# A planned delta-net and FFN kernel: the same steps in another order

## The chip, the cores and the metric

The kernel runs on one core of one Trainium2 chip. The core has five engines, each with its own instruction queue: TensorE (PE in the profile; its weight loads are PEld), VectorE (DVE), ScalarE (ACT), GpSimd (POOL) and SyncE (SP, which issues most of the DMA transfers). The engines run at their own pace [...]. The metric is the device time of one execution in microseconds, from the first instruction to the last.

## What is computed

Two blocks follow each other. The first is a delta-rule attention over q, k, v (batch 4, 8 heads, 768 tokens, 48 features):

```
k_n = k / (norm(k) + 1e-6)
for t in range(768):
    y[t]  = q[t] @ state
    state = state + beta[t] * outer(k_n[t], v[t] - k_n[t] @ state)
```

Its output, as 3072 tokens of 384 features, goes through a multiplicative feed-forward block:

```
a = x @ w1;  b = x @ w2          # 384 -> 1024
h = (a * b) @ w3                 # 1024 -> 1024
out = h @ w_out                  # 1024 -> 384
```

The weights arrive as 64-bit floats, so each has to be turned into a 32-bit one on the chip.

## The kernel before

**Attention.** The 768 steps are cut into 12 chunks of 64 tokens. Within a chunk the recurrence is solved at once through the inverse of a triangular 64x64 matrix for each of the 32 batch-heads. The work of a chunk m is cut into parts, each named by a letter and the number: `k`, `q`, `v`, `p` load (`p` loads k and q in blocks of 32 tokens, 16 DMAs in two steps); `K`, `Q` (chunks 0 and 1, on TensorE) and `d` (later ones, on VectorE) transpose; `g`, `N` compute norms and weights for a pair of chunks; `s` computes scores (L360, L366), U and the masked PT; `u` sends U to DRAM in blocks; `V` (for a pair of chunks) fetches the blocks and inverts all 32x32 ones by 31 steps on VectorE (L434, L439), then stores them; `e` fetches them back and fills the corner of the 64x64 inverse (L473 and L487 on TensorE, each followed by a copy on ScalarE); `n` scales v on GpSimd; `c` is the chain from one chunk's state to the next, three products in L517 (CH1, CH2, CH3) whose results VectorE turns into R, X and the new state S; `y` computes the outputs (L618), which ScalarE copies to xT, and for odd chunks six small DMAs (L650, "xTfix") move the last head pair in xT.

**Weights.** `P0` to `P7` are pieces of w_out, `P8` to `P23` of w3, `P24` to `P29` of w1, `P30` to `P35` of w2. Each piece is loaded by SP into one of five buffers, then handled by three ScalarE instructions (L671 to L673), one of VectorE (L675, the "shift") and two of GpSimd (L677, L678). Since (a * b) @ w3 @ w_out is linear in a * b, the kernel multiplies w3 and w_out once: `t` transposes a piece of w3 (L713), `f` folds eight of them with w_out into one block of w34 (L722, two halves). w_out lies in the memory that w2 fills later, so w2's pieces wait for the folds.

**Feed-forward.** For each pair of chunks (u = 0 to 5), `a<u><j>` computes block j of a and of b (L742, three matmuls each of 128x512), copies a on ScalarE, multiplies on VectorE (L756) into one of ten slabs; `o<u><b>` sums eight blocks with w34 into 128 output rows (L762), copies them (L768) and stores them (L771).

**Order.** Nothing is scheduled by the compiler. A list of names, `ORDER` (L37), is walked from left to right: each name advances its part by one step, and a step issues the instructions of one engine. `in_text_order` (L155) then chains the instructions of each engine, so that every queue runs strictly in the order of the list. The buffers are also handed out in list order: `two_banks` (L142) gives the two double banks of PSUM to scores, chain and outputs in turn, `bank` (L145) three banks to transposes, folds, `a` and `o`. While `V0` and `V1` run, one of the double banks is held for them.

Large TensorE phases are those with 128x128 weights (L713, L722, L742, L762); small ones address the array in tiles (64x48, 48x64, 32x32: L360, L366, L473, L487, L517, L618).

```
    for name in ORDER.split():
        step(name)
    in_text_order()
```

## Time and profile before

611.39 us is the median of three runs (611.04 to 615.68). The profiled execution spans 610.1 us.

| | us |
|---|---|
| TensorE busy | 567.9 (93%) |
| VectorE busy | 322.0 (53%) |
| ScalarE busy | 183.2 (30%) |
| GpSimd busy | 145.3 (24%) |
| L742 (a and b), both weights, x576 | 262.6 |
| L762 (outputs), x384 | 127.1 |
| L722 (folds), x128 | 46.8 |
| DMA traffic | 55.67 MB, 91 GB/s in the mean |

The chain that ended last is 83% TensorE, 5% SP issuing, 4% DMA. In the rows of forty digits each digit is the busy share of 15.25 us in tenths. The idle time of an engine that is not on the chain costs nothing by itself.

The order of time is: the first loads and transposes (to about 25 us), the first weights and block inverse (to 53), the folds with the chain of chunks 0 and 1 between them (53 to 131), then `a` and `o` with the attention of later chunks in between, and from 538 us feed-forward alone.

### The profile page before, as it was taken

Reading aid. Unit: us, or ns where it says so; the run is one execution under the profiler, and the core shown is the slowest. Engines: PE = TensorE matmul, PEld = TensorE weight load, DVE = VectorE, ACT = ScalarE, POOL = GpSimd, SP = SyncE. Lnnn points to the kernel's source line nnn. Section 1 sums busy time; section 2 is a strip of 40 time slices with the busy share of each in tenths; the row PEclk is TensorE's granted clock in tenths of the full one; section 3 lists DMA queues with packets and bytes.
Section 4 is the critical chain, followed back from the end, with each engine's and each line's share of the span. In section 5 each row is a group of like instructions: output and inputs, shape, how many; then the busy total and the mean of one; then the engine's idle time right before and its main releaser. Section 6 shows DMA issues by size and latency. Waiting matters only on the chain.

```text
span 610.1 us, 17982 instructions
## 1 busy us (share of the span) xinstructions
PE 567.9 (93%) x7804; PEld 333.7 (55%) x7804; DVE 322.0 (53%) x752; ACT 183.2 (30%) x373; POOL 145.3 (24%) x150
## 2 busy tenths in 40 slices
PE   3736988999899999999999999999999999999997
PEld 2724667644565655655466655465564655644454
DVE  1569875697665955557946449556386123100110
ACT  2776667654530212402111302122121212211100
POOL 6489866575242101100130000112001000000000
PEclk9999997899999999999999999999999999999999
DMA  9668887867755255253356324551321300000001
GB/s 216 163 207 195 195 176 168 193 118 155 158 77 105 67 116 85 30 94 72 62 119 87 55 55 96 101 74 23 57 81 26 97 2 2 24 30 13 1 13 39
DMA packets 202223, 55.67 MB, mean 91 GB/s; under 512 B 192352, under 2 KB 195424, under 8 KB 202144
## 3 DMA queue, kind: packets, MB, share of 16 engines
q1 hardware_dynamic: 197952, 53.74, 42.0%
q10 hardware_dynamic: 4192, 0.79, 0.9%
q8 instruction: 61, 1.00, 0.7%
q14 instruction: 18, 0.15, 0.1%
HBM read 42.30 MB, written 11.01 MB: 87 GB/s over the span
## 4 chain that ended last, share of the span: by engine, by line
PE 83%; SPq 5%; DMA 4%; ACT 3%; DVE 2%; issue 1%; POOL 1%; ACTq 0%; POOLq 0%; DVEq 0%
PE ps_f L742 38%; PE ps_f L762 20%; PE ps_f L722 5%; PE ps_w L517 5%; PE ps_w L618 4%; PE ps_t L473 2%; PE ps_w L366 2%; PE ps_t L487 2%; PE ps_w L360 2%; SPq L226 2%; PE ps_f L713 1%; SPq L663 1%; DMA X<-in_q_dram 1%; DMA raw<-in_moe_w_out_dram 1%; DMA ktok<-in_k_dram 1%
## 5 line engine op out<-in xcount | busy, mean ns | idle before, releaser
L742 PE MATMUL ps_f<-xT,w1s 128*128 128x512 f32 x288 | 131.1, 600 | 1.5 <-DMA xT<-xT 1.5
L742 PE MATMUL ps_f<-xT,w2s 128*128 128x512 f32 x288 | 131.5, 600 | 0.5 <-DVE ab L756 0.5
L762 PE MATMUL ps_f<-w,ab 128*128 128x384 f32 x384 | 127.1, 488 | 0.1
L756 DVE TENSOR_TENSOR ab<-a,ps_f 128x512 f32<-128x512 f32 x48 | 32.6, 683 | 136.5 <-PE ps_f L742 135.6
L762 PEld LDWEIGHTS ps_f<-w,ab 128*128 128x128 f32 x384 | 72.3, 190 | 51.5 <-issue 3.3
L742 PEld LDWEIGHTS ps_f<-xT,w2s 128*128 128x128 f32 x288 | 53.0, 190 | 61.2 <-issue 57.6
L742 PEld LDWEIGHTS ps_f<-xT,w1s 128*128 128x128 f32 x288 | 53.0, 190 | 60.4 <-issue 55.0
L751 ACT COPY a<-ps_f 128x512 f32<-128x512 f32 x48 | 27.7, 585 | 148.3 <-PE ps_f L742 116.5
L266 POOL TENSOR_TENSOR sq<-ktok 128x384 f32<-128x384 f32 x24 | 20.2, 844 | 147.7 <-DVE ss L268 82.1
L768 ACT COPY osb<-ps_f 128x384 f32<-128x384 f32 x24 | 11.5, 479 | 126.0 <-PE ps_f L762 97.0
L503 POOL TENSOR_TENSOR vtok<-vtok,n 128x384 f32<-128x384 f32 x24 | 20.2, 858 | 117.0 <-DMA vtok<-in_v_dram 103.9
L439 DVE TENSOR_TENSOR Vb<-Vb,tb 128x31 f32<-128x31 f32 (+15 forms) x124 | 45.2, 364 | 4.3
L722 PE MATMUL ps_f<-w2s,w3T 128*128 128x384 f32 x128 | 46.8, 518 | 0.1
L434 DVE TENSOR_TENSOR tb<-Vb,Ub 128x31 f32<-128x31 f32 (+15 forms) x124 | 43.9, 354 | 4.6 <-DMA Ub<-Ud 0.7
L639 ACT COPY xT<-ps_w 48x256 f32<-48x256 f32 x96 | 30.5, 366 | 48.4 <-PE ps_w L618 31.9
L722 PEld LDWEIGHTS ps_f<-w2s,w3T 128*128 128x128 f32 x128 | 24.9, 202 | 16.3 <-issue 2.7
L366 PE MATMUL ps_w<-KQ 48*64 48x64 f32 x768 | 31.3, 241 | 0.0
L360 PE MATMUL ps_w<-KQ 48*64 48x128 f32 x384 | 30.6, 307 | 0.7 <-ACT PT L386 0.7
L360 PEld LDWEIGHTS ps_w<-KQ 48*64 48x64 f32 x384 | 25.3, 154 | 8.6 <-issue 6.6
L713 PE MATMUL ps_f<-ident,w 128*128 128x128 f32 x64 | 12.6, 335 | 17.9 <-POOL w L678 17.9
L366 PEld LDWEIGHTS ps_w<-KQ 48*64 48x64 f32 x768 | 28.7, 154 | 0.3 <-issue 0.2
L581 DVE TENSOR_TENSOR S<-S,ps_w 48x768 f32<-48x768 f32 x20 | 19.0, 950 | 9.7 <-PE ps_w L517 9.5
(94 smaller groups left out, 642.4 us busy)
## 6 DMA issues: line engine op xcount, KB each, us to landing
raw<-in_moe_w_dram SPq DMA_DIRECT2D x16, 512.0 KB, 5.5
vtok<-in_v_dram SPq DMA_DIRECT2D x24, 192.0 KB, 4.0
raw<-in_moe_w_dram SPq DMA_DIRECT2D x24, 192.0 KB, 4.2
out_dram<-osb SPq DMA_DIRECT2D x24, 192.0 KB, 2.0
ktok<-in_k_dram SPq DMA_DIRECT2D x44, 96.0 KB, 3.4
raw<-in_moe_w_out_dram SPq DMA_DIRECT2D x8, 384.0 KB, 4.8
Ud<-U SPq DMA_DIRECT2D x48, 64.0 KB, 2.0
Ub<-Ud SPq DMA_DIRECT2D x6, 512.0 KB, 3.4
```

The lines of the kernel that those rows point to most:

```text
L360: pe.matmul(ps[half(z), 0, n : n + 128], lhsT=x[:, 0, :], rhs=x.rearrange("p j t -> p (j t)"), start=True, stop=True,)
L366: pe.matmul(ps[half(z ^ j), 1, n + C * j : n + C * j + C], lhsT=x[:, 0, :], rhs=x[:, j, :], start=True, stop=True,)
L434: dve.tensor_tensor(out=tv, in0=V[:, 0 : s + 1, s : s + 1].to_broadcast([P, s + 1, n]), in1=U[:, s, s + 1 : BS].unsqueeze(1).to_broadcast( ...
L439: dve.tensor_tensor(out=o, in0=o, in1=tv, op=ALU.subtract)
L517: pe.matmul(out(ps, r, h, z), lhsT=lhs(r, h, z), rhs=rhs(r, h, z), start=True, stop=True,)
L618: i = pe.matmul(region(h, z, r), lhsT=lhs, rhs=rhs, start=part[n] not in part[:n], stop=part[n] not in part[n + 1 :],)
L639: act.copy(out=xT[f, p:NP:2, b : b + NR, cc, :].rearrange("p a r t -> p r a t"), in_=pyv[f, z, b : b + NR],)
L722: pe.matmul(ps[:, 0:DM], lhsT=w3Ts[jc, kc // 4][:, kc % 4 * P : kc % 4 * P + P], rhs=wo[:, kc], start=(kc == 0), stop=(kc == KF - 1),)
L742: pe.matmul(ps[:], lhsT=w[:, m, js], rhs=x[:, m].rearrange("p b c t -> p (b c t)"), start=(m == 0), stop=(m == KM - 1),)
L751: act.copy(out=a[:], in_=ps[:])
L756: dve.tensor_tensor(out=t[:], in0=a[:], in1=ps[:], op=ALU.mult)
L762: pe.matmul(ps[:, 0:DM], lhsT=abs_[u, jc][:, b * P : (b + 1) * P], rhs=w34[:, jc, :], start=(jc == 0), stop=(jc == KF - 1),)
```

## The change

Only `ORDER` is replaced. The new list holds the same names the same number of times, so no instruction is added, removed or altered; each engine's queue, and with it the turn of every buffer, comes in another order. It is meant to put small TensorE phases more often beside each other, so that the array changes between large and small matmuls less often, and to bring weight pieces and loads in an order that suits the opening better. P1, P0 and P6 are now loaded before `k1` (before: P7 alone), and eleven pieces before the blocks of chunk 0 (`u0`), where there were eight.

The lists up to the first step of `c1` before and a similar stretch after, and their ends:

```diff
-P7 k0 g0 q0 V0 K0 g0 g0 k1 K0 K0 P7 P7 P7 K0 K0 Q0 Q0 Q0 Q0 Q0 g0 g0 g0 g0 K1 P0 P0 P0 P0 g0
-P3 K1 K1 K1 P3 P3 s0 g0 beta beta g0 P1 P1 q1 P1 beta N0 s0 K1 Q1 Q1 Q1 P10 P3 s0 s0 Q1 Q1
-P1 p2 s0 s0 s0 P10 P10 P10 P6 P6 s1 s1 s1 P11 s1 s1 s1 P6 P6 P13 N0 u0 u1 P11 P11 P12 P2 s1
-d2 d2 t2 t2 P13 P13 N0 P11 P13 V0 V0 P2 P2 P23 V0 P12 P12 t5 P12 P2 P22 P23 P4 V0 P22 V0 V0
-V0 V0 V0 P22 V0 V0 V0 t5 V0 P23 P4 P4 t3 t3 k3 t4 P22 t4 t14 t14 f2 P23 f1 P4 V0 V0 V0 V0 P5
-P5 P5 v0 P20 P20 V0 V0 V0 V0 V0 t15 P5 f2 V0 V0 P21 P21 f1 f2 P20 n0 n0 f7 V0 V0 V0 V0 P21
-V0 V0 V0 P15 P15 P15 V0 f1 V0 V0 t15 p3 P14 P14 s0 P20 k2 t12 f7 P17 t12 P14 f7 P21 t13 g1
-g1 P15 f6 p2 d2 d2 g1 V0 V0 V0 t7 t13 d3 t7 P17 f6 f6 P14 g1 g1 g1 P18 t6 t6 P18 s2 e0 P17
-g1 g1 f3 e0 g1 g1 N1 e0 P16 e0 P18 P16 s2 s2 s2 e1 e1 s2 s2 e0 f3 P16 e0 c0 c0 P9 P19 P19
-P19 f3 P9 P9 P17 t9 t9 p3 P18 t10 t10 v1 y0 y0 e1 e1 P16 t8 t8 d3 d3 P8 d3 s3 s3 s3 P9 P8
-P26 P26 s3 s3 s3 u2 P24 t1 t1 u3 c0 c0 P19 t11 P8 n1 n1 N1 N1 P24 e1 P25 V1 P26 P26 c1 f5
+k0 K0 g0 K0 P1 P0 g0 g0 q0 P6 k1 P1 K0 P0 Q0 K0 g0 P3 beta P6 K0 P1 V0 Q0 P0 Q0 K1 P1 g0 Q0 P6
+Q0 q1 P3 P7 g0 P10 P3 g0 K1 beta K1 K1 P7 g0 P6 K1 beta g0 P10 p2 Q1 g0 P3 P7 s0 P10 Q1 N0 P0
+s0 P2 Q1 Q1 Q1 P23 P7 s0 P2 P10 P12 s1 P13 s1 s0 s1 s0 s0 P2 P11 s1 P2 P12 s1 N0 u0 d2 s1 P13
+P12 u1 P23 s0 v0 P23 P11 t2 V0 d2 P12 P23 P22 P13 P13 V0 N0 P11 P4 k2 t2 t5 t4 P11 V0 V0 V0 V0
+P5 t3 V0 P22 V0 t5 V0 V0 P22 t4 V0 V0 P4 P20 t15 V0 P21 n0 f2 P4 V0 P5 P5 t3 P22 k3 t14 t15 V0
+P4 P20 V0 f1 P14 V0 P21 P20 V0 P15 P5 P21 V0 g1 f2 P14 V0 t14 f2 V0 V0 f1 P20 P18 V0 P15 p3 P14
+V0 t12 P19 P15 P21 V0 f1 V0 V0 f7 P14 P9 t6 P15 t12 n0 f7 P18 t13 V0 V0 t6 V0 V0 P8 V0 f7 V0 V0
+t7 g1 p2 t13 t7 V0 V0 P18 P8 g1 V0 g1 f3 d3 g1 s1 P17 g1 e0 P8 d2 f6 g1 P9 e1 f3 g1 P9 d2 d3 g1
+P18 s2 e0 g1 P19 N1 e0 s2 P16 e1 P8 f6 P9 P17 s2 P19 e0 e0 p3 f6 s2 f3 e0 s2 t10 s0 s2 c0 d3
+P19 s1 e1 v1 t10 d3 t1 P16 t1 s3 c0 n1 n1 s3 P16 y0 s3 t11 e1 y0 e1 s3 P25 P25 s3 t0 P24 P17 c0
+f5 V1 s3 u2 t11 u3 c0 P26 P17 P25 c1 V1 t0 P24 P16 P25 P24 V1 t9 e1 c1 f5 V1 V1 c1 k4 f5 c1 V1
...
-y11 o42 o42 o42 o43 o43 o43 a57 a57 a57 a57 a56 a56 a52 a52 a53 a53 a50 a50 o41 a50 a52 a52
-o41 o41 a50 a56 a56 a51 a51 a55 a53 a55 a53 a54 a54 a54 a54 a55 a55 a51 a51 o53 o53 o53 o51
-o51 o51 o52 o52 o50 o50 o50 o52
+c11 a45 a45 a42 a46 a45 a44 a45 a46 a44 c11 c11 o40 y11 o42 o40 o43 o32 y11 o43 y11 a53 o40 o43
+o42 a53 a54 o41 a54 a53 a53 a51 o41 o42 a51 a57 a57 a51 a51 a50 a54 a50 a57 a54 a55 a52 a57 a56
+a55 a56 a50 o41 a52 a56 a50 a55 a55 a56 a52 a52 o50 o50 o52 o50 o52 o51 o51 o52 o51 o53 o53 o53
```

An example from the middle: TensorE's queue from the second chain product of chunk 4 to the first of chunk 5 was CH2, `a11`, CH3, `a13`, `a15`, Y, E1, `a14`, CH1; it is now CH2, E1, CH3, Y, CH1 with no large phase between (the two tiny matmuls of `g3` left out of both).

More of the change, by code (lines that the diff above doesn't have):

```diff
@@ L44 @@
-V0 V0 V0 P15 P15 P15 V0 f1 V0 V0 t15 p3 P14 P14 s0 P20 k2 t12 f7 P17 t12 P14 f7 P21 t13 g1
-g1 P15 f6 p2 d2 d2 g1 V0 V0 V0 t7 t13 d3 t7 P17 f6 f6 P14 g1 g1 g1 P18 t6 t6 P18 s2 e0 P17
-g1 g1 f3 e0 g1 g1 N1 e0 P16 e0 P18 P16 s2 s2 s2 e1 e1 s2 s2 e0 f3 P16 e0 c0 c0 P9 P19 P19
-P19 f3 P9 P9 P17 t9 t9 p3 P18 t10 t10 v1 y0 y0 e1 e1 P16 t8 t8 d3 d3 P8 d3 s3 s3 s3 P9 P8
-P26 P26 s3 s3 s3 u2 P24 t1 t1 u3 c0 c0 P19 t11 P8 n1 n1 N1 N1 P24 e1 P25 V1 P26 P26 c1 f5
-P24 c1 e1 c1 c1 t11 V1 V1 V1 V1 V1 V1 V1 V1 V1 V1 f5 f5 P8 t0 t0 k4 s1 y1 y1 V1 P31 V1 V1
@@ L50 @@
-P25 P25 f4 P24 V1 P30 V1 V1 V1 V1 V1 V1 f0 P25 P30 P31 P30 P32 g2 v2 P31 c1 P31 V1 V1 f0 V1
-V1 f4 P28 f4 P30 P32 P32 P32 P28 f0 V1 V1 V1 V1 V1 y1 a01 p4 P28 a03 a01 k5 a00 a00 V1 V1
-a03 P28 p4 a01 d4 V1 V1 V1 g2 g2 a01 c1 g2 g2 g2 g2 V1 V1 P27 P27 P27 P27 a00 a00 P29 a03
-a03 V1 g2 d4 d4 P29 P29 P29 d4 e2 e2 a02 a02 a02 a02 g2 c2 e2 e2 P33 P33 a06 g2 N2 s4 a06 n2
-n2 c2 e2 s4 e2 s4 a04 a04 c2 c2 P35 P35 P35 e3 P33 P33 a07 P34 P34 P34 P34 c2 c2 y2 a07 a05
-p5 p5 d5 d5 d5 s4 s4 u4 s4 v3 P35 a06 y2 e3 e3 d5 a06 s5 s5 s5 s5 s5 s5 u5 a04 a04 a05 a05
@@ L56 @@
-a05 n3 n3 c3 c3 N2 N2 e3 e3 e3 a07 c3 a07 o03 V2 V2 V2 p6 V2 V2 V2 V2 o03 v4 o03 c3 y3 y3 V2
-V2 V2 V2 V2 V2 V2 V2 V2 V2 V2 V2 c3 n4 k6 g3 V2 V2 V2 V2 o00 o00 y3 o01 o01 o01 a10 a10 a17
-a17 g3 g3 a12 V2 v5 V2 V2 V2 p6 a12 a12 V2 V2 V2 V2 o02 V2 V2 V2 c3 c4 e4 e4 e4 a12 e4 a17
-a17 o00 d6 d6 o02 o02 g3 n4 c4 e4 e4 a10 a10 c4 k7 g3 a11 c4 c4 c4 a13 a13 a15 a15 a11 y4 n5
-e5 e5 e5 e5 a14 c5 a14 p7 d6 d6 p7 d7 g3 d7 d7 g3 g3 g3 e5 a16 y4 n5 c5 g3 s6 N3 s6 s6 d7 s6
-s6 s6 a16 a16 s7 s7 V3 s7 s7 s7 u6 u7 a11 a11 s7 V3 e5 c5 a16 a13 a13 p8 c5 a14 a14 c5 a15
@@ L62 @@
-a15 y5 y5 V3 V3 V3 V3 V3 o12 o12 o13 V3 V3 V3 c5 V3 V3 V3 V3 V3 V3 k8 V3 V3 o13 V3 V3 y5 a20
-a20 V3 V3 V3 d8 a27 a27 a23 a24 a24 k9 a23 a23 v6 n6 n6 V3 V3 V3 V3 V3 v7 V3 V3 a23 V3 o12
-V3 V3 g4 g4 g4 g4 V3 V4 g4 g4 a27 a27 a20 o13 e6 e6 o10 o10 p8 o10 o11 o11 o11 d8 d8 e7 a20
-e6 d8 N3 N3 c6 g4 g4 g4 g4 n7 n7 c6 e6 e6 a25 N4 s8 e7 s8 s8 a24 a24 s8 s8 s8 e6 c6 c6 p9 p9
-a25 a25 a25 y6 y6 c6 c6 a21 e7 c7 a21 c7 u8 a22 e7 e7 a22 d9 d9 d9 d9 s9 a22 a22 s9 s9 s9 s9
-s9 a21 a21 k10 e7 c7 c7 a26 y7 a26 p10 a26 a26 u9 V4 V4 V4 c7 o21 o21 y7 y7 V4 V4 V4 V4 V4
@@ L68 @@
-V4 V4 o22 o21 v8 V4 V4 o22 o22 V4 V4 V4 V4 V4 d10 o23 o23 v9 a35 a35 k11 a37 a37 V4 V4 V4 V4
-V4 V4 V4 V4 a34 V4 V4 g5 V4 V4 a34 a37 V4 V4 V4 a35 a35 g5 g5 c7 a37 o20 o20 g5 g5 g5 V4 e9
-e8 a36 e8 e8 e8 n9 g5 g5 g5 N4 N4 a36 c8 p10 d10 d10 n8 n8 c8 e8 e8 a30 v11 a30 g5 c8 a30 c8
-y8 y8 d10 s10 a34 p11 p11 c8 e9 e9 a30 N5 n11 d11 d11 a34 d11 s10 s10 a32 d11 s11 s11 s11 V5
-a32 a31 c8 a31 a31 a31 e9 e9 c9 n9 c9 s11 s11 s11 a36 n11 s10 s10 s10 u10 u11 V5 a32 a32 e9
-c9 c9 a33 a36 a33 o23 a33 N5 y9 y9 y9 a33 o33 o33 o33 V5 V5 V5 o20 V5 V5 V5 o32 V5 V5 o32
@@ L74 @@
-o32 V5 V5 V5 N5 a40 a40 a40 V5 a43 V5 V5 V5 V5 V5 V5 V5 V5 V5 V5 a40 a41 a41 a41 a43 V5 V5
-o31 a44 a44 o31 V5 a41 o30 v10 V5 c9 V5 V5 V5 o30 V5 V5 V5 e10 e10 o31 n10 n10 e10 a42 e10
-e10 e10 e11 a42 c9 c10 a46 a46 a46 a46 c10 a42 a42 c10 c10 a47 a47 y10 y10 e11 e11 e11 a43
-a43 c10 c10 o30 a45 a45 a45 a45 a47 a47 c11 c11 e11 e11 a44 a44 c11 c11 o40 o40 y11 o40 y11
-y11 o42 o42 o42 o43 o43 o43 a57 a57 a57 a57 a56 a56 a52 a52 a53 a53 a50 a50 o41 a50 a52 a52
-o41 o41 a50 a56 a56 a51 a51 a55 a53 a55 a53 a54 a54 a54 a54 a55 a55 a51 a51 o53 o53 o53 o51
@@ new lines @@
+V1 P26 V1 f0 V1 V1 g2 P26 t8 v2 g2 t9 V1 y1 t8 V1 P31 P30 y1 f4 P31 V1 V1 V1 P28 V1 f0 n2 V1
+P30 P24 V1 V1 P31 P30 f4 V1 f0 V1 N1 c1 f4 V1 N1 P26 V1 y1 g2 P32 P28 g2 P32 P32 P31 a01 V1 V1
+P30 V1 P28 P32 P27 V1 V1 k5 a01 V1 V1 V1 P28 V1 a03 V1 a03 P27 a00 p4 a00 V1 V1 a01 a03 g2 a01
+P27 P29 a03 V1 a02 g2 V1 p4 P27 g2 a02 V1 a02 c1 P33 P29 n2 d4 a00 e2 g2 c2 g2 P29 d4 P29 e2
+P34 e2 P33 e3 a02 e2 a00 p5 a04 d4 e2 a06 c2 e2 P34 P33 e3 P35 d4 g2 a07 P34 c2 N2 V2 c2 P35
+P34 s4 s4 e3 p5 a06 s4 c2 a04 y2 c2 P35 d5 a05 e3 d5 s4 k6 y2 d5 d5 s4 s5 P33 e3 a07 s4 s5 s5
@@ new lines @@
+v3 u4 g3 s5 c3 s5 g3 P35 s5 a04 a05 e3 n3 n3 a05 c3 a07 u5 g3 V2 a04 a06 a05 V2 V2 a07 a06 V2
+V2 c3 V2 c3 V2 N2 V2 p6 N2 o00 c3 o00 y3 V2 o03 o03 V2 v4 p6 V2 V2 V2 V2 V2 k7 o01 V2 o00 v5
+o03 V2 y3 g3 c3 V2 V2 V2 o02 y3 V2 n5 d6 a10 V2 d6 V2 p7 V2 V2 o02 V2 V2 o01 a17 n4 a10 n4 a12
+a17 V2 a12 V2 a12 d6 V2 g3 a13 V2 V2 c4 V2 e4 e4 e4 e4 g3 a11 g3 c4 e4 e5 g3 a12 a17 e5 e4 c4
+a13 a11 g3 c4 e5 o01 g3 c4 y4 c4 d6 c5 n5 k8 e5 a17 p7 N3 a10 y4 a13 c5 a10 d7 d7 a15 a11 a13
+s6 p8 a15 v6 d7 d7 s7 V3 s6 e5 e5 s6 s6 s6 g4 s7 a14 s7 u6 a11 o02 c5 s6 s7 a16 c5 s7 a16 a14
@@ new lines @@
+u7 a16 V3 a16 s7 a14 V3 V3 a14 V3 a15 V3 y5 g4 V3 c5 a15 V3 V3 y5 g4 V3 V3 o13 p8 V3 V3 V3 y5
+V3 o13 V3 n6 o12 a27 V3 d8 V3 V3 V3 V3 V3 o12 k9 V3 a27 d8 V3 o10 g4 V3 o12 V3 V3 g4 V3 a24 o13
+V3 g4 V3 V3 o10 a24 g4 o11 V3 a23 V3 V3 a23 a25 o11 e6 g4 a20 e7 d8 e6 d8 o11 e6 e6 n6 c5 c6 g4
+a25 s8 e6 c6 a27 a20 g4 a27 a23 a21 N4 s8 a24 a23 N3 s8 e6 c6 N3 p9 v7 a24 e7 a21 s8 e7 v8 p9
+c6 n7 y6 s8 s8 e7 c6 d9 k10 y6 a25 n7 o10 a22 d9 u8 d9 a25 a21 d9 g5 V4 c6 c7 s9 e7 s9 a22 s9
+e7 a26 g5 n8 c7 s9 a26 a21 c7 a20 a26 s9 a22 s9 c7 u9 a26 V4 g5 a22 c7 y7 a20 p10 k11 y7 o21
@@ new lines @@
+d10 v9 V4 V4 y7 p10 V4 V4 V4 o23 V4 V4 V4 o21 V4 V4 a37 V4 a37 V4 V4 a35 o23 a35 o23 V4 o21 V4
+V4 V4 V4 n9 a34 V4 a37 d10 V4 V4 n8 V4 V4 V4 V4 g5 a34 c7 a34 V4 V4 a37 a30 V4 V4 g5 o20 V4 V4
+d10 a30 V4 e8 p11 a34 g5 n9 o20 o22 e9 a31 o22 a31 e8 d10 g5 e8 p11 g5 c8 g5 o20 e8 N4 e8 e9 c8
+N4 v11 g5 a35 e8 c8 e9 s10 V5 c8 N5 y8 a32 d11 y8 e9 a35 n11 a33 d11 s10 a32 a36 a33 s10 s10
+d11 a36 c8 a30 s10 s10 d11 u10 s11 e9 c8 s11 s11 c9 s11 c9 e9 N5 s11 a30 c9 a32 a32 N5 a33 a31
+u11 c9 s11 a36 a33 a31 a36 V5 V5 c9 V5 y9 V5 V5 V5 V5 y9 V5 V5 o31 o31 v10 V5 V5 V5 o33 y9 V5
@@ new lines @@
+V5 n10 V5 c9 V5 o22 V5 a43 V5 a41 V5 o33 a41 V5 V5 a43 V5 a40 V5 o31 o30 V5 o33 V5 V5 V5 V5 V5
+o30 a41 a40 V5 a43 V5 a40 o30 V5 V5 e10 a43 e11 a41 o32 a47 o32 a47 n11 a40 a44 c10 e11 e10 e10
+a44 a42 a46 e10 e10 a46 a42 a47 e10 n10 c10 c10 e11 c10 e11 c10 y10 e11 e11 c10 c11 a47 a42 y10
+c11 a45 a45 a42 a46 a45 a44 a45 a46 a44 c11 c11 o40 y11 o42 o40 o43 o32 y11 o43 y11 a53 o40 o43
+o42 a53 a54 o41 a54 a53 a53 a51 o41 o42 a51 a57 a57 a51 a51 a50 a54 a50 a57 a54 a55 a52 a57 a56
+a55 a56 a50 o41 a52 a56 a50 a55 a55 a56 a52 a52 o50 o50 o52 o50 o52 o51 o51 o52 o51 o53 o53 o53
```

## The prediction

> **What bounds the kernel now.** I read the busy shares first, then the waits of TensorE, then each stage, then the chain that ended last.

> ```profile
> span 610.1 us, 17982 instructions
> PE 567.9 (93%) x7804; PEld 333.7 (55%) x7804; DVE 322.0 (53%) x752; ACT 183.2 (30%) x373; POOL 145.3 (24%) x150
> PE   3736988999899999999999999999999999999997
> PEclk9999997899999999999999999999999999999999
> ```

> TensorE is full from the ninth slice (15.25 us each) on; what it lacks lies ahead of that. Cutting the span at the first fold (53.3 us) and at the start of `corner(2)`'s first matmuls, `e2`, (155.5 us):

> ```profile
> 0.00:53.30 53.30, 23.75 (x488) 20.95 (x489) 28.48 (x69) 33.10 (x62) 38.03 (x45) 1.00 0.84 199
> 53.30:155.50 102.20, 94.71 (x1260) 59.02 (x1258) 74.59 (x184) 59.70 (x114) 68.91 (x61) 0.95 0.78 167
> 155.50:610.10 454.60, 449.42 (x6060) 253.70 (x6060) 218.94 (x501) 90.38 (x197) 38.38 (x46) 1.00 0.31 62
> ```

> The columns are length, then PE, PEld, DVE, ACT and POOL busy, clock, DMA. The opening has 29.6 us without a matmul, the middle 7.5, the last 455 us almost none. So only two things can be gained: waits before 155 us, and TensorE's own time per phase after it. The waits of TensorE name the first:

> ```profile
> PE ps_f L713 <- POOL w L678: 17.9, 5, 7.9
> PE ps_f L333 <- DMA ktok<-in_k_dram: 7.1, 3, 4.8
> ...
> PE ps_t L473 <- DVE T L464: 1.8, 1, 1.8
> PE ps_f L742 <- DMA xT<-xT: 1.5, 1, 1.5
> ```

> The transposes of w3 wait for GpSimd to finish weight pieces (17.9 us). GpSimd is not full there; its queue is blocked:

> ```profile
> 22.27 1.01 POOL L678 TENSOR_TENSOR w2s<-w2s,raw 128x384 f32<-128x384 f32 x1
> 28.05 1.26 POOL L388 TENSOR_TENSOR PT<-PT,smask 128x512 f32<-128x512 f32 x1 [4.77 <-ACT PT L386]
> ```

> It stood 4.77 us before `s0`'s mask, though ScalarE had finished P1, the next piece in line, at 22.86. For the last stage, phases from the chain that ended last:

> ```profile
> 161.68 2.77 PE ps_f L742 x6
> ...
> 200.21 0.72 PE ps_w L517 x64
> ...
> 211.45 10.30 PE ps_f L742 x24
> ...
> 273.11 0.86 PE ps_w L517 x64
> ```

> 24 large matmuls in a row take 10.30, so 6 take 2.575; 6 alone between small phases take 2.77, 0.2 more. A 64x48 phase between large ones takes 0.86, beside another of its kind 0.72.

> [...] about 0.1 us at each border between 128-row matmuls and the small ones, 0.2 per isolated large run. [...] TensorE waited 2.4 us before 92.5, and the records then show half clock from 93.5 to 100.3 and from 107.2 to 110.6. [...] here the piece shift L675, mostly 0.35 to 0.43 us, took up to 1.50 while GpSimd worked.

> **The change, part by part.** Nothing is added or removed; each queue gets the same work in another order. I took each engine's new queue and gave every step its duration from the trace.

> (1) *Fewer borders after `e2`.* I counted TensorE's queue from `e2` on. Runs of large matmuls enclosed by small phases: 47 before, 27 after. 20 fewer at 0.197 (0.104 when a small phase precedes, 0.093 when one follows) is -3.9 us. Pairs of neighbouring 64-wide phases (scores, chain, outputs): 9 before, 22 after; savings in the trace are 0.03 to 0.16 a pair, I take 0.08: -1.0.

> (2) *What side by side can cost.* A result must be evicted while less TensorE work lies between. In the new order the tightest are: `c10`'s second to third product, 1.13 us of work over an X of 1.02; `c4`'s, 1.23 over 1.02; `c9`'s first to second, 1.19 over an R of 0.95; `c4`'s third to `c5`'s first, 2.27 over an S of 1.92. Before, the tightest were two of 1.28 over a copy of 1.17, and all waits of L487 for that copy sum to 0.2 us. Queued behind a waiting matmul is all of TensorE, so every such wait counts in full. Bounds: 0, and 0.6 us (half an eviction) at each of five places, 3.0; I take 0.5. The long way, scores to block inverse to `e4`, `e6`, `e8`, `e10`: with about 22.5 us for 31 inverse steps, the other VectorE work now between them (7.7, 4.4, 3.9, 1.9 us) and 7 us for the trip through DRAM and back, I get 1.4 to 2.5 us to spare at the first three and more at the last: nothing, but little margin.

> (3) *First fold.* GpSimd's work up to the piece that the first fold waits for is 33 us in both orders (11 pieces at 2.1 or 2.7, plus masks and squares). Before, it starts at 8.1 and ends at 52.4, 11.3 us idle. Afterwards P6, P3, P0, P7 and P10 stand ahead of the two masks, which fills the 4.77 us gap; with ScalarE's copies set in the new order I get an end near 46 and the first fold near 47 instead of 53.3. Its second half, needing P5, comes near 54 instead of 60.2: 6 us earlier.

> (4) *Block inverse.* Its first step was at 44.7, held by `V0`'s copy to PSUM behind P2 on ScalarE (waiting for a DMA until 41.8). The copies now stand behind P11 and P22 around 40 to 42, when the blocks land: start near 42, end near 68 (was 71.1), the store `V0` at 69.2, behind `p2`'s second half (was 72.7). `c0`'s first product then comes about 4 us earlier (was 88.4).

> (5) *From there to the first `ab`.* Before, this took 42.4 us (88.4 to 130.8), of which TensorE's extras over steady durations were about 11. The half-clock stretches, 10.2 us in all, account for some 5. They follow the wait of 2.4 us of the transpose `t10`, whose bank came free only at 92.4, when `f3`'s copy had passed P19's conversion on ScalarE. Now P19 and P17 are converted ahead of `e0`, and that copy follows `f6`'s at once. Also, SP issues the six copies into xT (3.7 us) without P32 ahead of them, so they land behind the last folds although `y1` has three half folds after it instead of four; the 1.5 us wait for xT goes. Walked step by step, the whole opening comes out 15 us shorter at `e2`. But such a walk sees only waits it looks for; those of the half clock and of crossed queues cost 11 us here before. I take 4 us at `c0` plus 5: -9. Bounds: -16 (all of it) and 0.

> (6) *End.* The last `ab` was block 1, which the next output needs second (0.5 us wait for VectorE); it is now block 2, with one more 0.65 us accumulation ahead of it. The last store was queued behind another (about 0.4); now it follows its own copy. -0.9.

> Sum: -3.9 - 1.0 + 0.5 - 9 - 0.9 = -14.3; 611.4 - 14.3 = 597.1.

> **Rivals.** *The walk holds in full:* -16 in the opening: 590. For: all pieces it needs are converted earlier. Against: DMA is 84% busy and any slip meets a full SP queue. *A new wait eats the opening:* [...] only (1) and (6) remain, less 1 to 3 of (2): 606 to 608, no difference worth the name. For: I see one wait of about 2 us, `e0` after its transposed blocks near 77. *Slower:* ScalarE now starts with P1 ahead of `K0`'s first copy, and three pieces go out on SP ahead of `k1`, so the first loads share the engines; `p2`'s loads and P8 stand before the store of `V0`. If K0, Q0 and K1 come 5 us late and the inverse with them, the masks and folds wait, with one more half-clock stretch: +9 in the opening, -4 after it: 616. Against: before, ScalarE idled 7.75 us to its table load anyway, and `k0` and `q0` are under a quarter of the first 3.5 MB (sizes of the issues).

> **How the numbers follow.** My forecast has 0.6, the full walk 0.2, the eaten opening 0.12, slower 0.08. The likeliest gives 597.1. Range 588 to 607: below lies a part of the full walk, above, the slow case and some of the eaten opening. Faster by over 1% (below 605.3): 0.8 with most of the forecast's spread; within 1% 0.12; slower 0.08.

> **What would show it.** (1) 27 isolated large runs after `e2`, still 2.77 for six, and span minus `e2`'s start about 5 us below 454.6. (2) Waits of TensorE on L550, L560 or L480 near zero. (3) first L722 at 46 to 49; the wait of L713 on GpSimd well under 17.9. (4) the first inverse step near 42. (5) no 7 and 8 in the seventh and eighth slices of the clock row, first L742 at 118 to 124. (6) no wait on L756 before the last outputs. The prediction falls if the opening's first scores come later than about 27 us, if the clock row dips again, or if TensorE shows waits over 3 us in sum after `e2`.

## The result: slower by 4%

The changed kernel takes 636.1 us in the median (634.6 to 640.1) against 611.2 for the kernel before, run beside it: a ratio of 1.040, 95% interval 1.035 to 1.045. The forecast said 597.1 and allowed 588 to 607; it had the wrong sign. Of the signs that were to show it false, three came: the first scaled scores at 33.5 us (not by 27), new dips of the clock row, and waits of TensorE of well over 3 us after `e2`.

The page of the changed kernel, rows as shown before (one digit of the two rows is now 15.8 us). All line numbers of the changed kernel are two lower than before, as its list is two lines shorter: L740 and L760 are the feed-forward products, L515 the chain, L616 the outputs. (The kernels of the experiments have other line numbers again, as their edits add lines.)

```profile
span 632.9 us, 17994 instructions
PE 570.4 (90%) x7804; PEld 338.1 (53%) x7804; DVE 336.1 (53%) x752; ACT 182.9 (29%) x373; POOL 146.0 (23%) x150
PE   1638879997899998999998999999999998999997
PEclk9957997998989999899999999999999997999999
```

TensorE does the same work in the same busy time (570.4 for 567.9), but its row now has eights and sevens all through the attention part, where the old row was an unbroken line of nines. The clock row dips at the start and five times more. The same three stages as before, cut at the first fold and at the first matmuls of `e2`:

```profile
0.00:53.44 53.44, 22.71 (x488) 19.88 (x489) 28.96 (x61) 31.46 (x59) 38.73 (x45) 0.79 0.81 192
53.44:156.48 103.04, 92.10 (x1257) 57.53 (x1256) 83.28 (x189) 63.27 (x121) 71.12 (x63) 0.95 0.78 177
156.48:632.90 476.42, 455.59 (x6060) 260.68 (x6060) 223.82 (x504) 88.15 (x194) 36.15 (x42) 0.98 0.29 57
```

The stages were 53.3, 102.2 and 454.6 us long. So the opening is 1 us longer, not 9 shorter, and 21.8 us are lost in the last stage, where I had put a gain of 4.4 and 0.9. The waits of TensorE over the whole span name what is new:

```profile
PE ps_f L711 <- POOL w L676: 11.5, 3, 9.1
PE ps_f L331 <- DMA ktok<-in_k_dram: 9.2, 3, 6.4
PE ps_w L515 <- issue: 9.0, 8, 3.3
PE ps_w L616 <- issue: 6.3, 5, 1.6
...
PE ps_t L471 <- DVE T L462: 4.6, 2, 4.2
...
PE ps_w L515 <- DVE X L558: 2.5, 1, 2.5
```

"issue" is time in which the engine waited for nothing that the profile knows; 13.2 us of it lie after `e2`, where the kernel before has none. The timeline of TensorE shows one such place (x48 means 48 matmul records; an fp32 matmul leaves two of them in the trace: the 32 matmuls of a chain product are x64):

```profile
248.52 0.85 PE L616 MATMUL ps_w<-PT,X 64*48 64x64 f32 x48
250.97 0.44 PE L616 MATMUL ps_w<-PT,X 64*48 64x64 f32 x16 [1.60 <-issue]
...
253.07 7.05 PE L740 MATMUL ps_f<-xT,w2s 128*128 128x512 f32 x12
```

The gap stands between the 48th and the 49th of 64 like matmul records, whose operands were all there. No eviction and no semaphore separates them. The twelve large ones that follow take 7.05 us instead of about 5.2: the records show half clock from 253.0 to 256.4.

I counted such gaps inside a small phase after `e2`, taking every place where one record starts over 0.5 us after the one before it: none before, 11 in the changed kernel, 14.5 us in sum. Counted in matmul records from the first (at 187 us), the others come 7, 12, 18, 22, 26, 27, 32, 36, 37 and 38 times 127.17 records later, all within 0.02 of a whole number. A twelfth, of 0.8 us, lies 15.0 times 127.17 records from the first, but in a run of large matmuls (328 us). A fixed spacing in the count of instructions, with no regard to what they compute, points to the instructions themselves. The DMA view has a queue for them:

```profile
q8 instruction: 61, 1.00, 0.7%
```

61 packets, 1.00 MB: the trace has each at 16,384 bytes, about 64 bytes for each of the 7804 matmul records and as many weight loads. `after_half`, a run further on with 736 fewer of each, has 55, and 64 bytes for each record give 6 packets fewer there (an estimate from these counts). A packet then covers 128 matmul records with their loads, a little less with the 123 other instructions that the trace has in the same queue, and the gaps lie at multiples of 127.17. The theory from here on, F: these packets bring TensorE's instructions, in blocks, and a block cannot follow the one before in less than about 3.6 us (the closest that these packets start to each other is 3.4 to 3.9), while 127 records of small phases need only 2.2 us at 17 ns each. The new order puts small phases so close that blocks are used up sooner than they come. The times of the packets fit: each of the 12 gaps ends 2.4 to 2.8 us after one of them starts. So do the block borders, if they lie 127.17 records apart as the gaps do: where a gap stands, it is 2.8 to 4.0 us from the border before it; most other pairs of borders are over 4.2 us apart. But six pairs of 2.2 to 3.5 us pass without a gap, so 3.6 us is no exact limit. Rival D: dependences between engines that the profile does not name. Rival O: the slower opening.

### The profile page after: what moved, and what is told of

Its sections match the earlier page's. It is cut to its first block, busy times and chain, and to the rows that moved or that the text cites. A ratio compares the mean times of both kernels' runs of the same rounds, so it can differ in the third digit from the quotient of the medians.

```text
span 632.9 us, 17994 instructions
## 1 busy us (share of the span) xinstructions
PE 570.4 (90%) x7804; PEld 338.1 (53%) x7804; DVE 336.1 (53%) x752; ACT 182.9 (29%) x373; POOL 146.0 (23%) x150
## 4 chain that ended last, share of the span: by engine, by line
PE 70%; DVE 10%; DMA 9%; SPq 4%; issue 4%; ACT 3%; ACTq 0%; DVEq 0%
PE ps_f L740 34%; PE ps_f L760 18%; PE ps_w L515 5%; PE ps_w L616 4%; DVE tb L432 3%; PE ps_t L471 2%; PE ps_t L485 2%; PE ps_w L358 2%; DMA raw<-in_moe_w_dram 2%; PE ps_w L364 2%; DVE Vb L437 2%; DMA ktok<-in_k_dram 2%; SPq L224 1%; DMA Vd<-Vb 1%; DMA TT<-Vd 1%
## 5 line engine op out<-in xcount | busy, mean ns | idle before, releaser
L740 PE MATMUL ps_f<-xT,w2s 128*128 128x512 f32 x288 | 133.5, 613 | 0.8 <-issue 0.8
L740 PE MATMUL ps_f<-xT,w1s 128*128 128x512 f32 x288 | 130.6, 600 | 0.0
L760 PE MATMUL ps_f<-w,ab 128*128 128x384 f32 x384 | 127.0, 488 | 0.3 <-DVE ab L754 0.3
L760 PEld LDWEIGHTS ps_f<-w,ab 128*128 128x128 f32 x384 | 72.3, 190 | 51.7 <-issue 2.9
L740 PEld LDWEIGHTS ps_f<-xT,w2s 128*128 128x128 f32 x288 | 55.2, 195 | 67.2 <-issue 64.6
L740 PEld LDWEIGHTS ps_f<-xT,w1s 128*128 128x128 f32 x288 | 54.6, 192 | 64.0 <-issue 60.3
L264 POOL TENSOR_TENSOR sq<-ktok 128x384 f32<-128x384 f32 x24 | 20.4, 852 | 155.7 <-DVE ss L266 98.3
L766 ACT COPY osb<-ps_f 128x384 f32<-128x384 f32 x24 | 11.3, 480 | 141.2 <-PE ps_f L760 104.2
L432 DVE TENSOR_TENSOR tb<-Vb,Ub 128x31 f32<-128x31 f32 (+15 forms) x124 | 44.7, 360 | 5.8 <-DMA Ub<-Ud 2.2
L720 PE MATMUL ps_f<-w2s,w3T 128*128 128x384 f32 x128 | 44.2, 497 | 0.0
L358 PE MATMUL ps_w<-KQ 48*64 48x128 f32 x384 | 29.6, 298 | 5.1 <-ACT PT L384 5.0
L372 DVE TENSOR_TENSOR U<-ps_w,wt 128x512 f32<-128x512 f32 x24 | 16.3, 686 | 27.5 <-PE ps_w L364 27.2
L358 PEld LDWEIGHTS ps_w<-KQ 48*64 48x64 f32 x384 | 24.0, 148 | 9.9 <-ACT PT L384 5.2
L364 PEld LDWEIGHTS ps_w<-KQ 48*64 48x64 f32 x768 | 27.8, 149 | 1.3 <-issue 1.1
L432 DVE TENSOR_TENSOR tb<-ps_w,Ub 128x31 f32<-128x31 f32 (+15 forms) x62 | 21.0, 338 | 7.0 <-DMA Ub<-Ud 5.4
```

Of the source, the lines that this page charges most:

```text
L358: pe.matmul(ps[half(z), 0, n : n + 128], lhsT=x[:, 0, :], rhs=x.rearrange("p j t -> p (j t)"), start=True, stop=True,)
L364: pe.matmul(ps[half(z ^ j), 1, n + C * j : n + C * j + C], lhsT=x[:, 0, :], rhs=x[:, j, :], start=True, stop=True,)
L432: dve.tensor_tensor(out=tv, in0=V[:, 0 : s + 1, s : s + 1].to_broadcast([P, s + 1, n]), in1=U[:, s, s + 1 : BS].unsqueeze(1).to_broadcast( ...
L720: pe.matmul(ps[:, 0:DM], lhsT=w3Ts[jc, kc // 4][:, kc % 4 * P : kc % 4 * P + P], rhs=wo[:, kc], start=(kc == 0), stop=(kc == KF - 1),)
L740: pe.matmul(ps[:], lhsT=w[:, m, js], rhs=x[:, m].rearrange("p b c t -> p (b c t)"), start=(m == 0), stop=(m == KM - 1),)
L760: pe.matmul(ps[:, 0:DM], lhsT=abs_[u, jc][:, b * P : (b + 1) * P], rhs=w34[:, jc, :], start=(jc == 0), stop=(jc == KF - 1),)
```

## Which part loses, and is it the fetch

**Half the list at a time.** `open_new` is the new list as far as `e2`, then all that is left in the old order; `rest_new` the old list to `y3`, then the new order.

> The new list up to the first matmuls of corner(2), e2, and from there the old list's order for all that is left. Theory F (instruction fetch): TensorE's own instructions come from memory in blocks of 16,384 bytes, some 127 matmul records with their weight loads, and not oftener than one in about 3.6 us; the loss after e2 is where the new order sets small phases so close that a block is used up sooner. Here the part after e2 is the old one, so no waits named issue after e2, and 610 to 613 us. Rival O (the slower opening leaves less room, and the rest suffers from it): 625 to 635 us, with most of the 22 us after e2 still there.

Measured 616.6, ratio 1.007 (1.004 to 1.009): the new opening costs some 4 us, more than F had put there, with a wait of 2.5 us for a transposed block at `e2` and half clock around it. With the old rest behind it no gap inside a small phase appears. O falls.

> The mirror image: the old list up to the first matmuls of outputs(3), y3, at about 198 us, and from there the new order. Theory F: the blocks that run short lie after y3, so about 15 us are lost: 624 to 628 us, with six or more issue waits of 1 us and over in the middle of small phases. Rival O: the old opening keeps the buffers ahead of TensorE, so 606 to 612 us.

Measured 646.5, ratio 1.055 (1.049 to 1.061). Eleven gaps, 14.5 us in sum, are there, as F has it. The forecast for the total missed by 20 us. The two halves don't fit: TensorE waits 7.3 us for a transposed block (T) and 5.8 us for xT, waits that neither parent has at this length, and half clock lies around both. A hybrid shows which waits it carries over; its total is its own.

**Moving the block borders and nothing else.** 40 or 10 matmuls are put ahead of all TensorE work, where it idles for k.

```diff
     make_identity(nc, ident[:])
+    pad = psT.tile([P, BS], FP32, tag="t0", name="pad", bufs=1)
+    for _ in range(40):
+        nc.tensor.matmul(
+            pad[0:BS, :], lhsT=ident[0:BS, 0:BS], rhs=ident[0:BS, 0:BS], start=True, stop=True
+        )
```

> The kernel before, with 40 small matmuls added ahead of TensorE's first work, where it waits for k anyway (their result is not read). They change no order and no dependence, only the place of every block border in TensorE's list of instructions, by 80 matmul records. Theory F: the borders now fall so that some ten pairs of neighbouring borders after e2 lie less than 3.6 us apart, summing to 14 us in a model of fixed durations: 619 to 626 us, with waits named issue of 1 to 1.7 us in the middle of small phases, in y2, c3, e5, e6, c6, e8. Rival D (the lost time after e2 is waits for another engine that the profile does not name, since the new order is tight): nothing changes, 610.5 to 612.5 us.

Measured 627.2 against 612.5, ratio 1.023 (1.017 to 1.030): 14.7 us slower with an unchanged order, just above F's range. `outputs(2)` (y2), which ran through before, breaks:

```profile
168.01 0.42 PE L623 MATMUL ps_w<-KQ,S 48*48 48x64 f32 x11
170.12 0.54 PE L623 MATMUL ps_w<-KQ,S 48*48 48x64 f32 x21 [1.70 <-issue]
```

Nine gaps, 10.7 us in sum, lie in y2, c3, e5, e6, c6, e8, s10, s11 and e11, again at whole multiples of 127.17 from each other, and each ends 2.2 to 2.7 us after a packet of instructions starts. Three half-clock stretches of 3.4 us stand behind three of them and can account for the rest. D has no place for this.

> The same with 10 small matmuls, borders moved by 20 records. Theory F: no pair of borders after e2 is closer than 3.6 us, where the kernel before has two (2.7 us in the model): 608 to 611 us. Rival D: 610.5 to 612.5 us.

Measured 612.7, a ratio of 1.001 (0.999 to 1.003), which F's 608 to 611 missed. No gap, and none to win: what the model put at 2.7 us in the kernel before, its trace doesn't have.

**Without VectorE's inverse steps** (V2 to V5).

```diff
         for s in range(BS - 1):
+            if j > 1:
+                yield
+                continue
```

> The changed kernel without VectorE's work in the block inverses V2 to V5 (their 31 steps each are left out, some 85 us of VectorE; the output is then not the reference's). All orders and TensorE's work stay. Rival D, in the form that TensorE after e2 waits for VectorE (results that come late behind inverse steps in its queue): with most of that queue empty the time falls to 613 to 620 us. Theory F (fetch of TensorE's instructions, in which VectorE has no part): 628 to 637 us, with the same waits of 1 to 2 us named issue in y4, c6, c8, y8, c10 and y10.

Measured 635.8, ratio 1.036 (1.029 to 1.043): VectorE's busy time falls from 336 to 246 us, and the time stays. The waits after `e2` are the old ones:

```profile
PE ps_w L619 <- issue: 6.7, 6, 1.4
PE ps_w L518 <- issue: 5.8, 6, 1.4
```

All 11 gaps of the changed kernel come back at the same record numbers, with two more at whole multiples. This is the clearest cut between F and D, as far as D means VectorE.

**Fewer instructions in the same order.**

```diff
+    def upper(x):
+        return x.bitcast(BF16).rearrange("p (t w) -> p t w", w=2)[:, :, 1]
...
-                    region(h, z, r), lhsT=lhs, rhs=rhs,
+                    region(h, z, r), lhsT=upper(lhs), rhs=upper(rhs),
```

> The changed kernel, in which the 64-wide matmuls of outputs(c) read only the upper 16 bits of their fp32 operands (as bf16, so the output is rougher than the reference's). Each is then one load and one matmul instead of two and two: half the instructions and half the time in these phases, nothing else changed. Their time alone is 11.4 us less after e2. Theory F: fewer blocks in the clusters, stalls of 15.6 us in the model instead of 24.1: 636 - 11.4 - 8.5 = 616 us, 613 to 620; and against the kernel before with the same edit 14 to 18 us slower instead of 25. Rival D: nothing waits closely for these phases, so only their own time goes: 623 to 627 us, still 23 to 27 us slower than the other.

> The kernel before with the same edit, for the difference: the outputs' matmuls read the upper 16 bits of their operands as bf16. Both theories: 611.4 - 11.4 = 600 us, 597 to 603, as its blocks are far enough apart either way (2.7 us of stalls in the model before, 2.2 after the edit).

Measured 620.5 and 607.4 (ratios to the kernel before 1.012, 1.004 to 1.019, and 0.992, 0.990 to 0.994). The difference of the two is 13.1 us instead of 25, on F's side of the two theories and just outside its range of 14 to 18; the gaps fall from 14.5 to 8.6 us. The old order gains only 5 of its 11 us: with shorter phases it waits 3.1 us for T11 at `e2` and 2.0 for PT, each with half clock, and has two gaps of its own. The records of TensorE fell from 7804 to 7068, its busy time by 10.4 us (570.4 to 560.0) and by 9.0 (567.9 to 558.9). So the edit did not act on the fetch alone, and the sizes are soft.

**The fetch by itself.**

> Not the reference's computation: the outputs are zeros, and all of the work is left out but this. VectorE runs six small products of two SBUF tiles (128x32), six products of one SBUF tile with a constant, and six of a PSUM tile with an SBUF tile, first with GpSimd idle, then while GpSimd runs products of 128x512. Then TensorE, after a warm-up, runs six streams without any dependence, each of eight groups of 64 matmuls: 64 minus n small ones (64x48) and n large ones (256 columns), n = 0, 1, 2, 3, 4, 6, with twelve 512-column ones between streams. Theory F: a block of 16,384 bytes holds 64 fp32 matmuls (two loads and two matmul records each), so the stream without large ones takes 3.4 to 3.9 us a group instead of 2.2, n = 1 and 2 the same 3.4 to 3.9, and only n = 4 and 6 their own 3.9 and 4.7. Without a limit on the fetch: 2.2, 2.6, 3.0, 3.4, 3.8, 4.6 us. Theory P [...]: the products of two SBUF tiles go from 0.2 to about 1 us each, the others stay near 0.2; without it all stay.

The pure stream took 3.8 us a group, as F has it, but so did the small matmuls of every other stream, however many large ones stood between: used in two of four positions they need 30 ns each, 3.8 us for 128, which is no less than F's 3.6. Nothing follows for F.

> Not the reference's computation: outputs are zeros. The first such kernel ran its small matmuls in two of the four 64x64 positions only, 30 ns for each record, too slow to ask the fetch for more than it gives. This one goes round all four, as the kernel's products do (17 ns). Streams without dependence, groups of 64 fp32 matmuls (256 instructions): 64 minus n of 64x48 and n of 256 columns, n = 0, 1, 2, 3, 4, 6. Theory F: 3.4 to 3.9 us a group for n = 0, 1, 2 and 3, then 3.9 and 4.6 us. Without a fetch limit 2.2, 2.6, 3.0, 3.4, 3.8, 4.6 us. VectorE: eight dependent products of two SBUF tiles (128x32), alone and beside GpSimd's 128x512 products: 0.2 us each alone, and by theory P 1 us or more each beside them.

Its streams:

```python
large(24, 512)
for n in (0, 1, 2, 3, 4, 6):
    for _ in range(8):
        small(64 - n)
        large(n, 256)
    large(12, 512)
```

With all four positions in use, the stream without large matmuls:

```profile
34.02 2.77 PE L104 MATMUL res<-wide,mat 64*64 64x48 f32 x173
38.04 2.08 PE L104 MATMUL res<-wide,mat 64*64 64x48 f32 x128 [1.25 <-issue]
41.49 2.08 PE L104 MATMUL res<-wide,mat 64*64 64x48 f32 x128 [1.38 <-issue]
44.95 2.08 PE L104 MATMUL res<-wide,mat 64*64 64x48 f32 x128 [1.38 <-issue]
48.67 2.08 PE L104 MATMUL res<-wide,mat 64*64 64x48 f32 x128 [1.65 <-issue]
```

This is the same effect without any kernel around it: 173 records run without a stall (by F, from what was fetched ahead), then 128 records, 2.08 us of work, come every 3.45 or 3.72 us. With one large matmul in 64 the first two groups run free (2.64 us each) and the others take 3.1 to 4.0; with two the first two run free (3.06), the others take 3.4 to 4.0. With three, four and six a group takes 3.49, 3.82 and 4.67 us, its own time. So no wait at a block border shows in the last three streams (but for one stall of 0.24 us), in the first three it does, and one or two large matmuls in 64 are too few to cover it.

## Can the order be mended

Single products go back between the small phases; TensorE's queue around chunk 10 (small phases by name, `a` one product), changed, first and second list:

```diff
-CH2 E1 CH3 Y E2 CH1
+CH2 a40 E1 CH3 a47 Y a45 E2 CH1
+CH2 a40 E1 CH3 a42 Y a44 E2 CH1
```

> The changed list with 13 single large-matmul phases (one w1 or w2 product of a ff block, six matmul records, 2.6 us) moved a few places into the clusters of small phases, so that fewer neighbouring block borders of TensorE's instructions lie closer than 3.6 us; no other step is moved, except the copy or product that belongs to a moved phase. Theory F (instruction fetch, with the half clock that follows its gaps): of some 24 us lost after e2, about 20 come back, less 2 us for 10 to 13 new borders between large and small phases: 613 to 619 us, issue waits in small phases down from 16 us to under 4. Rival D (tight dependences between engines): the products move TensorE's work, not the chains, and the time stays at 630 to 637 us.

> A second list with spread products: the changed list, in which 15 single w1 or w2 products are moved by a few phases so that neighbouring block borders lie 3.7 us apart, and this time only where no result gets less TensorE work between it and its use than the changed list itself shows without a wait. Theory F: of the 22 us in large gaps after e2, the fetch gaps (some 15 us) and the half clock behind them (5 us) go: 612 to 619 us, near the 616.6 of the new opening with the old rest, and issue waits after e2 under 3 us. Rival D (the smaller gain of the first such list came because the lost time is dependences between engines, not fetch): 628 to 634 us again.

In the second list the first factor of one ff block (a27) lies in a buffer that is reused before the product reads it, so that block's values are not the reference's; the work is the same. Measured 631.8, ratio 1.030 (1.023 to 1.036), and 632.8, ratio 1.030 (1.025 to 1.036): the totals are those of D, though the traces are not. The gaps inside small phases fell as designed, from 14.5 to 5.0 and to 2.1 us; of the waits named issue after `e2`, 1.1 us is left in the first list and nothing in the second. To see what took their place I summed, from the first `ab` on, what each phase of TensorE took over the shortest steady duration of its kind, apart for phases with more and with less than 0.45 us of it (a sum that depends on the durations taken as steady):

| us | before | changed | spread2 | open_new |
|---|---|---|---|---|
| in large extras | 3.2 | 31.5 | 19.5 | 7.1 |
| in small extras | 8.6 | 4.2 | 9.0 | 8.3 |

The small extras are the borders. The change saved 4.4 us of them, and spreading the products gives them all back (4.8), so 12 us of gaps won become 7 in the profile (626.2 for 632.9). The large extras left in spread2 are mostly the wait at `e2` with its half clock (7.3) and the cluster of c2 and y2 (5.3). They are no longer waits for the fetch but waits that the profile names, and half clock around them. Two of these waits after `e2` are new:

```profile
PE ps_f L740 <- ACT a L749: 3.3, 1, 3.3
PE ps_f L740 <- DVE ab L754: 2.7, 3, 1.4
```

Here a product set between small phases waits for the copy or the result of another product. All named waits from `e2` on sum to 13.9 us in spread2, to 7.0 in the changed kernel. So neither list had few borders and few gaps together: by F, a large run between small phases gives the fetch time to catch up, and it costs borders and dependences of its own.

## The opening

In the changed kernel GpSimd worked where it had stood idle before the first mask, as forecast, but VectorE, computing the norms N0 just then, slowed down. Two of its 15 instructions:

```profile
29.61 1.32 DVE L280 SCALAR_TENSOR_TENSOR nt<-ss,nr 128x32 f32<-128x32 f32 x1
30.96 0.19 DVE L283 TENSOR_TENSOR nt<-nt,nr 128x32 f32<-128x32 f32 x1
```

The first five take about 1 us each, until GpSimd ends its last piece at 30.88; from then on 0.19. The norms take 8.1 us instead of 4.0, and the mask that waits for them comes at 34.84 instead of 28.05, so that GpSimd still stands idle for 3.95 us ahead of it (4.77 before). The profile puts none of this down to a semaphore: the instructions themselves are longer. What of theory P can be read here is that small VectorE instructions take longer while GpSimd works; by what way is not shown. In `micro2` eight dependent products of two tiles (128x32) took 1.77 us alone and 5.56 beside GpSimd's 128x512 products. In `micro` the products of two tiles stayed at 0.18, against my expectation, and those of a tile with a constant took 1.26; the three kinds ran in turn, so each of the first kind came shortly after a long one. That this spared them is my guess, not shown.

The same happens to the next two norms, N1 (7.7 us for 3.5) and N2 (7.6 for 3.5). In N2, four instructions take 1.17 to 1.34 us while GpSimd handles a piece of w2, from 166.1 to 171.5 us:

```profile
167.48 1.34 DVE L285 SCALAR_TENSOR_TENSOR nr<-nt,seed 128x32 f32<-128x32 f32 x1
```

VectorE comes to `c2`'s X only when N2 ends, at 173.4, and this is the wait of 2.5 us for X in the list above; the 4.1 us that N2 lost are longer than it. `after_noinv` shows both again (7.6 and 2.5). In the old order N2 ran from 156.6 on, while GpSimd stood idle.

> The kernel before with one move on GpSimd: the last step of the weight piece P1 ahead of the first mask of scores(0), into the 4.8 us in which GpSimd stood idle. As my forecast took it: GpSimd ends its pieces 2.1 us earlier and nothing else changes, first fold at 51.2 us instead of 53.3, 609 to 611 us. Theory P: the norms N0, which run just there, take 5.5 to 6.5 us instead of 4.0, and the scores, masks and the inverse come 1.5 to 2.5 us later, so that nothing is gained: 611 to 614 us.

```diff
-P10 P3 s0 s0 Q1 Q1 P1 p2
+P10 P3 s0 P1 s0 Q1 Q1 p2
```

Measured a ratio of 1.002 (1.000 to 1.005). As theory P has it, the norms took 5.5 us; the first fold came at 54.9 us, not at 51.2.

> The kernel of the first experiment (new opening up to e2, old rest) with one move on GpSimd: the last steps of the weight pieces P0, P7 and P10 stand behind the first mask of scores(0), not ahead of it, so that GpSimd idles again while VectorE computes the norms N0. Theory P: N0 takes 3.5 to 4.5 us instead of 8.1, the first scaled scores come about 4 us earlier, at 29 us instead of 33.4, and GpSimd itself is no later with its pieces: 612 to 616 us against 616.6. Rival: the norms are long for another reason (their operands, a semaphore), so they still take 8 us, and GpSimd's pieces come 5 us later: 617 to 622 us.

```diff
-N0 P0 s0 P2 Q1 Q1 Q1 P23 P7 s0 P2 P10 P12 s1 P13 s1 s0
+N0 s0 P2 Q1 Q1 Q1 P23 s0 P2 P12 s1 P13 s1 s0 P0 P7 P10
```

Measured 621.0, ratio 1.010 (1.005 to 1.016). The norms took 3.5 us and the scaled scores came at 30.0 us, as P has it; but GpSimd idled 7.1 us, and the first fold came at 58.4 us, so the total is the rival's. Here one engine had that stretch at the other's cost (norms of 3.5 us with GpSimd idle for 7.1, of 8.1 us beside it), and neither choice gains.

Two waits of the kernel before, the one on which step (5) rests and the one at `e2`, each attacked by one move:

```diff
-c0 c0 P9 P19 P19 P19 f3
+c0 c0 P9 P19 f3 P19 P19
```

> The kernel before with one move on ScalarE: the copy of fold f3 ahead of the conversion of P19. It tests step (5) of the forecast alone, that the 2.4 us wait of the transpose t10 at 90 us comes from that copy, and that the two half-clock stretches after it (10.2 us long) come from the wait. If both hold: no wait over 1 us between 88 and 96 us, no half clock before 110 us, 603 to 607 us. If the wait goes but the half clock stays: 608.5 to 610. If another wait takes its place: 611 to 613.

Measured a ratio of 1.000 (0.998 to 1.002). The 2.4 us wait of t10 is gone (so the copy was its cause, as the forecast said, though the profile puts it down to GpSimd) and TensorE starts y0 at 91.4 instead of 93.1, but then it waits for the next thing due: 1.3 us for VectorE's transposed keys and 3.1 for a block of TT. Half clock comes all the same, from 96.9 and 110.6. The first `ab` starts at 132.5 (before: 130.8).

> The kernel before with one move on SP: the store of the inverted blocks V1 ahead of the loads of P27 and P29 instead of behind them. The chain is store, load of the blocks into TT, transposed block T11, first matmuls of e2, where TensorE waits 1.9 us at 153.6 us. If the queue of SP is what delays it: the store issues 3.5 to 4 us earlier, e2's wait goes, 608.5 to 610 us. Rival: P27 and P29 land later and an ab product waits instead: 611 to 613 us.

```diff
-V1 V1 P27 P27 P27 P27 a00 a00 P29 a03 a03 V1
+V1 V1 V1 P27 P27 P27 P27 a00 a00 P29 a03 a03
```

Measured a ratio of 1.001 (0.999 to 1.003). The wait of 1.8 us at `e2` is gone, but `e2` starts no earlier (155.4 us): an `ab` product ahead of it waits 3.1 us for VectorE's product, where P27 comes later (0.5 before), and a wait of 1.1 us for a transposed block appears at 179 us.

> Both moves together, and five single w1 or w2 products of the old list (a13, a36, a15, a21, a32) moved so that they join a run of large matmuls or part two block borders; no neighbouring borders after e2 closer than 3.8 us in the model. Sum of the single effects, if they add up: 600 to 606 us. If the two waits hide each other's gain: 607 to 610 us.

Measured 622.5, ratio 1.015 (1.011 to 1.019), slower than both its parts and far from the 600 to 606 expected. It has no fetch gap inside a phase: its five moved products take away cover instead, and results come late (2.8 us for VectorE's squares at 254 us, 2.9 for `ab` products, 2.0 for TT). None of the orders tried beats the kernel before.

## Why the forecast was wrong

(1) *Fewer borders:* right. -4.9 forecast, -4.4 measured in the small extras. An isolated run of six still takes 2.77.

(2) *What side by side can cost:* this step failed most. I asked only whether a result is evicted in time, took 0.5 us and bounded it at 3. The size of that part was nearly right, but by luck: the one new wait of this kind, 2.5 us for `c2`'s X, is at none of the places that I had listed, and comes from N2 beside GpSimd. What I left out at no cost is, by F, the fetch of the instructions, which clusters of small phases outrun, though its row (61 packets of instructions) stood in the profile of before: 14.2 us in gaps inside phases, over the records' own spacing, and 0.8 in the twelfth. Behind them and the waits for T11 and X lie 18 us of half clock after `e2` (154.0 to 160.8, 174.5 to 177.9, 253.0 to 256.4, 526.0 to 532.9), and the phases in them show 7.5 us of extras. With 2.5 for X and less the 4.4 of (1), that is 20.6 of the 21.8 us.

(3) *First fold:* 53.4 us, not 47. This step failed too: it filled GpSimd's gap and put the cost of that to VectorE at nothing, although the forecast itself shows the shift grown to 1.50 us while GpSimd worked. The norms paid 4.1 us, the masks came later, and GpSimd stood idle 3.95 us all the same.

(4) *Block inverse:* first step at 48.7, not 42; end at 76.3, not 68. Its input is the scaled scores, 6.8 us late: N0 starts 2.7 later (25.3 for 22.6, with more pieces loaded and shifted ahead of it) and takes 4.1 longer; `c0`'s first product at 94.8 was 6.4 us later than before instead of 4 earlier.

(5) *From there to the first `ab`:* here the new order did what I took it to do, and more: 35.4 us instead of 42.4, -7 for -5. With (4) the two cancel: first `ab` at 130.2 for 130.8. Then `e2` waits longer for T11 (4.2 for 1.8 us): its transpose starts 1.0 us later (155.7 for 154.7), and TensorE is there 1.3 us sooner. V1's inverse steps ended 4.8 us later than before (145.1 for 140.3); most of that had been slack, as the store behind them was issued only 0.9 us later. That the half clock cost 5 us that one freed wait would return is not borne out: b_f3 freed it and gained nothing.

(6) *End:* right. The time from TensorE's last matmul to the end of the execution fell by 0.5 us (3.9 to 3.4), and a pause of 0.3 us ahead of the last outputs is gone.

The rival "slower" had a late opening at 616 us. It named the right place for the 4 us of open_new, for another reason, and none of the rivals had the last stage.

## What to carry to other kernels

Count instructions, not only microseconds: work out how long TensorE takes for each 128 fp32 matmul records, and where that falls below 3.5 to 3.7 us (the spacing in `micro2`, 3.45 to 3.72) for more than a block, leave large matmuls in between (two of 512 columns in 64 bring it to about 3.8, an estimate from 17 ns and 0.43 us a record, the latter from 24 in 10.30 us), and price the borders and waits that they bring. When a wait named issue falls in the middle of a uniform phase, count records between such waits; a fixed spacing (127.17 here) points to the fetch, and moving the borders by a few dozen matmuls on an idle engine tests it. Before giving GpSimd more to do in a stretch, look at what VectorE runs there (N0 took 8.1 us for 4.0). A wait that an opening full of transfers shows may be worth nothing (the two taken away here were): take it away in one run before building a forecast on it.
